# A row of exponentials times its inverse sum: the scaling of the last query tile moves from VectorE to ScalarE

## The chip, the cores and the metric

The kernel runs on one core of a Trainium2 chip. Its engines are TensorE (PE; PEld is its weight load), VectorE (DVE), ScalarE (ACT), GpSimd (POOL) and SyncE (SP), which here only issues transfers. Each works through its own queue in order and waits on semaphores for the others. The metric is the time of one execution on the device in microseconds (us).

## What is computed

Attention with rotary positions over 2 batches x 8 heads x 576 positions x 64, whose output, with the heads side by side, goes through a dense mixture of 4 experts. All in float32.

```python
scores = scale * np.matmul(q_rot, k_rot.transpose(0, 1, 3, 2))
scores = scores - np.max(scores, axis=-1, keepdims=True)
attn = np.exp(scores)
attn = attn / (np.sum(attn, axis=-1, keepdims=True) + 1e-09)
attn_out = np.matmul(attn, v)
# x: 1152 tokens x 512, p: the experts' normalised weights
for e in range(E):
    out += p[:, e:e + 1] * (np.maximum(x @ w1[e], 0.0) @ w2[e])
```

## The kernel before

Two heads are worked on together as a pair, so that each batch has four pairs. The 576 query rows of a head are 4 tiles of 128 and a rest of 64. A pair has nine units of work: units 0 to 7 are the full tiles of its two heads, and unit 8, `TAIL`, holds the 64 rest rows of both heads in one tile of 128 rows.

A unit goes through a chain. `scores` (L282, TensorE) writes a 128x576 tile to PSUM; `max` (L293, VectorE) takes the row maxima; `exp` (L301, ScalarE) writes the exponentials `e` to SBUF and adds their row sums into one column of `total`; `turn_e` and `turn_x` (L315 and L341, TensorE) transpose `e`; `high` and `low` (L332 on ScalarE, L336 on VectorE) split the transposed tile into a high and a low part, `high_x` and `low_x` (L344, L348) do so for the last 64 columns of two units; `values` (L365 to L368, TensorE) multiplies by the values; `lower` and `add` (L372 on ScalarE, L376 on VectorE) put the two halves of that product together.

Units 0 to 7 are divided by their sums only after that: `inverse` (L382, L383) turns `total` into 1/(total + 1e-9), `spread` (L392, VectorE) copies the inverses out to 512 columns, `rows` (L398, TensorE) transposes them, `divide` (L403) multiplies. Unit 8 is divided before its transposes: `scale` (L387) multiplies the SBUF tile `e` of 128x576 by the last column of `total`, one number per partition, in place. Its transposes (L315 again) wait for that; `copy_e` and `copy_x` (L351, L354) bring the result to SBUF for `tail_values` (L417).

The order of all this is written out by hand: every step has a due time in a table, `ALONE` or `BESIDE`, and one heap hands the steps to the engines' queues in order of due time. The first batch runs alone (`ALONE`); the second runs between the matmuls of the experts on the first batch's tokens (`BESIDE`; L601 to L603 with the relu L561, then L576 to L578), and the experts on the remaining tokens come last. GpSimd meanwhile rotates the queries and keys of the pairs to come and subtracts the high part of weights from the weights (L142, behind ScalarE's copy L135); towards the end it also makes sums of tokens (L644, L649) which ScalarE copies (L656). In this document "tail 1" to "tail 8" are the unit 8 of the eight pairs in order of time. Steps that belong to `TAIL` get their due times so:

```python
for key in (
    "copy_e", "copy_x", "inverse", "scale", "spread", "rows", "divide", "out_high", "out_low",
    "tail_values", "tail_high", "tail_low",
):
    at(key, getattr(self, key))
```

In `ALONE` the due times within unit 8 are exp 0.566, inverse 0.587, scale 0.712, tail_turn 1.096, spread 3.143; in `BESIDE` exp 0.181, inverse 0.243, spread 0.555, scale 0.697, tail_turn 1.093.

Of the kernel before, what the change touches and what calls it, by code (L numbers as in the profile page):

```python
# [16 lines left out]
AF = mybir.ActivationFunctionType  # L17
# [38 lines left out]
def kernel(  # L56
# [17 lines left out]
    nc = tc.nc  # L74
# [11 lines left out]
    TAIL = 2 * NR  # L86
# [58 lines left out]
    class Pair:  # L145
# [238 lines left out]

        def scale(self):
            e = self.e[TAIL]
            nc.vector.tensor_scalar_mul(e, e, self.total[:, TAIL:])  # L387

        def spread(self):
            self.rep = apool.tile([P, NR, 2, D], F32, tag="rep", name=f"rep{self.nm}")  # L390
# [727 lines left out]
```

## Time and profile before

| | |
|---|---|
| runs without a profile | 580.94, 579.58, 579.60 us; median 579.6 |
| the profiled execution | 582.67 us, of which the span of the trace is 580.9 |
| TensorE busy | 545.8 us (94%) |
| VectorE busy | 335.1 us (58%) |
| ScalarE busy | 279.1 us (48%) |
| GpSimd busy | 334.7 us (58%) |
| chain that ended last | TensorE 73%, VectorE 9%, ScalarE 8%, GpSimd 4%, transfers 3% |

The span is cut to what the engines did; 1.77 us lie around it. Busy shares are means over stages that differ: attention alone until about 107 us, attention beside experts until about 360, experts to the end. The last line follows the execution back from its last instruction, at each step to what released it.

### The profile page before, as it was taken

How to read it: one execution, taken by the hardware profiler on the slowest of the kernel's cores; microseconds unless marked ns; L12 is line 12 of the kernel's file. 1: busy time of each engine (PE TensorE's matmuls, PEld its weight loads, DVE VectorE, ACT ScalarE, POOL GpSimd, SP SyncE). 2: the span in 40 equal slices, each digit the busy share in tenths (PEclk: the TensorE clock that was granted, in tenths of full speed). 3: DMA queues.
4: the chain of work that ended last, by engine and by line, in shares of the span. 5: the costliest groups of instructions: out<-in, count | busy, mean ns of one | idle time of the engine just before them, and what ended most of it. 6: DMA issues, size and time to landing. Idle time of an engine off the chain costs nothing.

```text
span 580.9 us, 8599 instructions
## 1 busy us (share of the span) xinstructions
PE 545.8 (94%) x3229; PEld 477.9 (82%) x3229; DVE 335.1 (58%) x590; ACT 279.1 (48%) x545; POOL 334.7 (58%) x228
## 2 busy tenths in 40 slices
PE   3898888899999999999999998889999999999996
PEld 3787877788888888888888887877899899889985
DVE  5588798434362434444335445876678587777702
ACT  4688778456344554555535543443244335324400
POOL 6999992357824673478334484456663683565300
PEclk9799999999999999999999999998999999999999
DMA  5245031064125222441242124422243123223002
GB/s 149 63 120 138 3 101 60 3 184 151 66 64 157 72 74 62 113 136 49 73 136 73 45 64 140 150 54 92 74 113 106 55 77 125 73 72 109 2 0 90
DMA packets 42459, 50.67 MB, mean 87 GB/s; under 512 B 7218, under 2 KB 32050, under 8 KB 42418
## 3 DMA queue, kind: packets, MB, share of 16 engines
q1 hardware_dynamic: 41618, 49.38, 28.6%
q10 hardware_dynamic: 800, 0.75, 0.5%
q8 instruction: 25, 0.41, 0.3%
q14 instruction: 16, 0.13, 0.1%
HBM read 43.34 MB, written 2.36 MB: 79 GB/s over the span
## 4 chain that ended last, share of the span: by engine, by line
PE 73%; DVE 9%; ACT 8%; POOL 4%; DMA 3%; issue 2%; SPq 0%; ACTq 0%; POOLq 0%; DVEq 0%
PE po L816 6%; PE po L818 6%; PE po L817 6%; PE sc L282 5%; PE ph L601 4%; PE ph L603 4%; PE ph L602 4%; PE p L737 4%; PE p L738 4%; PE p L739 4%; PE po L578 4%; PE po L576 4%; PE po L577 4%; PE pp L315 4%; ACT e L301 3%
## 5 line engine op out<-in xcount | busy, mean ns | idle before, releaser
L142 POOL TENSOR_TENSOR wl<-wr,wh 128x1024 fp32r<-128x1024 f32 x64 | 155.1, 2427 | 130.6 <-ACT wh L135 125.1
L135 ACT ACTIVATE wh<-wr 128x1024 fp32r<-128x1024 f32 x64 | 67.4, 1054 | 38.8 <-PE po L578 16.6
L293 DVE TENSOR_REDUCE mx<-sc 128x1 f32<-128x576 f32 x72 | 54.2, 753 | 39.6 <-PE sc L282 39.1
L142 POOL TENSOR_TENSOR sl<-sf,sh 128x1024 fp32r<-128x1024 f32 x16 | 38.5, 2404 | 50.1 <-ACT sh L135 50.1
L816 PE MATMUL po<-wh,hH 128*128 128x512 f32 x160 | 63.0, 394 | 2.8 <-DVE hL L777 2.8
L301 ACT ACTIVATE e<-sc,mx 128x576 f32<-128x576 f32 x72 | 53.3, 741 | 24.9 <-DVE mx L293 24.4
L818 PE MATMUL po<-wh,hL 128*128 128x512 f32 x160 | 62.8, 392 | 0.0
L817 PE MATMUL po<-wl,hH 128*128 128x512 f32 x160 | 62.8, 392 | 0.0
L562 DVE SCALAR_TENSOR_TENSOR hL<-ph,hH 128x512 fp32r<-128x512 f32 x32 | 22.1, 692 | 61.0 <-ACT hH L561 61.0
L315 PE MATMUL pp<-ident,e 128*128 128x128 f32 x288 | 45.3, 281 | 7.8 <-DVE e L387 5.6
L576 PE MATMUL po<-wh,hH 128*128 128x512 f32 x128 | 52.3, 409 | 0.0
L601 PE MATMUL ph<-xH,wh 128*128 128x512 f32 x128 | 51.5, 402 | 0.0
L332 ACT ACTIVATE ptH<-pp 128x512 fp32r<-128x512 f32 x64 | 38.1, 595 | 25.3 <-PE x L365 17.2
L578 PE MATMUL po<-wh,hL 128*128 128x512 f32 x128 | 50.3, 393 | 0.0
L603 PE MATMUL ph<-xH,wl 128*128 128x512 f32 x128 | 50.2, 392 | 0.0
L577 PE MATMUL po<-wl,hH 128*128 128x512 f32 x128 | 50.0, 391 | 0.0
L602 PE MATMUL ph<-xL,wh 128*128 128x512 f32 x128 | 50.0, 391 | 0.0
L516 DVE TENSOR_TENSOR sf<-wr 128x256 f32<-128x256 f32 x32 | 39.4, 1272 | 18.3 <-DMA wr<-in_moe_w_dram 18.3
L336 DVE TENSOR_TENSOR ptL<-pp,ptH 128x512 fp32r<-128x512 f32 x64 | 43.9, 686 | 10.2 <-ACT ptH L332 9.8
L775 ACT ACTIVATE hH<-p 128x320 fp32r<-128x320 f32 x64 | 27.2, 436 | 41.0 <-DVE p L767 40.9
L135 ACT ACTIVATE sh<-sf 128x1024 fp32r<-128x1024 f32 x16 | 17.0, 1062 | 61.8 <-DVE sf L516 61.8
L315 PEld LDWEIGHTS pp<-ident,e 128*128 128x128 f32 x288 | 34.4, 143 | 14.5 <-issue 4.1
(161 smaller groups left out, 1370.9 us busy)
## 6 DMA issues: line engine op xcount, KB each, us to landing
wr<-in_moe_w_dram SPq DMA_DIRECT2D x68, 512.0 KB, 3.6
k2T<-kT SPq DMA_DIRECT2D x14, 288.0 KB, 3.9
rawv<-in_v_dram SPq DMA_DIRECT2D x8, 256.0 KB, 2.8
out_dram<-acc SPq DMA_DIRECT2D x8, 256.0 KB, 2.6
rawk<-in_k_dram SPq DMA_DIRECT2D x7, 256.0 KB, 4.2
rawq<-in_q_dram SPq DMA_DIRECT2D x7, 256.0 KB, 3.2
rawv<-in_v_dram SPq DMA_DIRECT2D x16, 32.0 KB, 2.5
tabs<-in_rope_dram ACTq DMA_DIRECT2D x1, 320.0 KB, 3.5
```

The costliest lines, as they stand in the source:

```text
L135: nc.scalar.activation(out=hi, in_=src, func=AF.Copy)
L142: eng_l.tensor_tensor(out=lo, in0=src, in1=f32(hi), op=ALU.subtract)
L315: nc.tensor.transpose(pp[:, c * P : (c + 1) * P], self.e[u][:, c * P : (c + 1) * P], ident)
L576: nc.tensor.matmul(po[t], lhsT=sH, rhs=wH, start=(f == 0), stop=False)
L577: nc.tensor.matmul(po[t], lhsT=sH, rhs=wL, start=False, stop=False)
L578: nc.tensor.matmul(po[t], lhsT=sL, rhs=wH, start=False, stop=(f == NF - 1))
L601: nc.tensor.matmul(o, lhsT=wH[:, kt], rhs=xh, start=(kt == 0), stop=False)
L602: nc.tensor.matmul(o, lhsT=wH[:, kt], rhs=xl, start=False, stop=False)
L603: nc.tensor.matmul(o, lhsT=wL[:, kt], rhs=xh, start=False, stop=(kt == KT1 - 1))
L816: nc.tensor.matmul(po[t], lhsT=sH, rhs=wH, start=(f == 0), stop=False)
L817: nc.tensor.matmul(po[t], lhsT=sH, rhs=wL, start=False, stop=False)
L818: nc.tensor.matmul(po[t], lhsT=sL, rhs=wH, start=False, stop=(f == NF - 1))
```

## The change

`scale` is issued to ScalarE as a copy with a scale per partition, in place of VectorE's multiplication. The due time stays; only the queue is another. Eight instructions change, one per pair.

```diff
         def scale(self):
             e = self.e[TAIL]
-            nc.vector.tensor_scalar_mul(e, e, self.total[:, TAIL:])
+            nc.scalar.activation(out=e, in_=e, func=AF.Copy, scale=self.total[:, TAIL:])
```

TensorE's, GpSimd's and SyncE's queues are the same instruction by instruction. On ScalarE at tail 3 (names carry the number of the pair and the unit, so `e_2_8` is the tail of pair 2; `wh` is a copy of weights):

```order
 L332 ACTIVATE ptH_2_6_1129<-pp_2_6_1124 128x4x128
 L301 ACTIVATE e_2_8_1164,total_2_843<-sc_2_8_1139,mx_2_8_1155 128x576
+L387 ACTIVATE e_2_8_1164<-e_2_8_1164,total_2_843 128x576
 L332 ACTIVATE ptH_2_6_1129<-pp_2_7_1159 128x4x128
 L135 ACTIVATE wh_0_0_1_1188<-wr_0_0_1_972 128x1024
```

The new instruction stands between the exponential of unit 8 and the high part of unit 7, with the weight copy behind that. On VectorE at tail 3:

```order
 L382 TENSOR_SCALAR total_2_843<-total_2_843 128x9
 L383 RECIPROCAL total_2_843<-total_2_843 128x9
-L387 TENSOR_SCALAR e_2_8_1164<-e_2_8_1164,total_2_843 128x576
 L293 TENSOR_REDUCE mx_3_0_1199<-sc_3_0_1172 128x1
 L336 TENSOR_TENSOR ptL_2_6_1130<-pp_2_7_1159,ptH_2_6_1129 128x4x128
```

The maxima of the next pair's first unit now follow the inverse directly. On VectorE at tail 8, in the second batch, the scaling stood behind `spread`:

```order
 L348 TENSOR_TENSOR ptX_3_6_3737<-x_112,ptX_3_6_3737 64x256
 L392 COPY rep_3_3830<-total_3_3389 128x512
-L387 TENSOR_SCALAR e_3_8_3804<-e_3_8_3804,total_3_3389 128x576
 L354 COPY at_3_8_3860<-x_112 64x128
 L376 TENSOR_TENSOR xf_3_3536<-x_112,tmp_3_3_3869 64x256
```

It no longer has `spread` in front of it; on ScalarE it stands behind L656 and ahead of `copy_e` (L351).

## Rows read from the trace of the kernel before

**Rows 1.** Stretches: length, busy us (instructions) of PE, PEld, DVE, ACT, POOL, clock, DMA.

```profile
58.00:81.00 23.00, 19.87 (x163) 17.80 (x163) 19.40 (x33) 19.21 (x46) 22.08 (x21) 1.00 0.18 44
240.00:300.00 60.00, 60.00 (x347) 51.28 (x345) 24.67 (x43) 30.05 (x56) 33.80 (x23) 1.00 0.33 98
```

**Rows 2.** Groups by line: count, busy us, mean ns, idle before and its releasers.

```profile
L387 DVE TENSOR_SCALAR e<-e,total 128x576 f32<-128x576 f32 x8 | 6.1, 766 | 0.1
...
L382 DVE TENSOR_SCALAR total<-total 128x9 f32<-128x9 f32 x8 | 7.4, 929 | 2.6 <-ACT e L301 2.5
...
L301 ACT ACTIVATE e<-sc,mx 128x576 f32<-128x576 f32 x72 | 53.3, 741 | 24.9 <-DVE mx L293 24.4
...
L406 ACT ACTIVATE xH<-xf 128x512 fp32r<-128x512 f32 x8 | 5.0, 622 | 1.1 <-DVE xf L403 1.1
```

**Rows 3.** Timeline, tail 3: start, us, engine, line, operation, [idle before <-releaser]; GpSimd, VectorE, TensorE.

```profile
77.77 2.39 POOL L142 TENSOR_TENSOR wl<-wr,wh 128x1024 fp32r<-128x1024 f32 x1
...
78.12 2.08 DVE L382 TENSOR_SCALAR total<-total 128x9 f32<-128x9 f32 x1
...
84.11 2.32 DVE L392 COPY rep<-total 128x512 f32<-128x512 f32 x1
...
87.84 0.63 PE L398 MATMUL pr<-ident,rep 128*128 128x128 f32 x4 [1.15 <-DVE ptL L336]
```

**Rows 4.** Timeline, tail 2: VectorE, ScalarE and TensorE.

```profile
56.84 1.51 DVE L387 TENSOR_SCALAR e<-e,total 128x576 f32<-128x576 f32 x1
...
59.11 0.74 ACT L301 ACTIVATE e<-sc,mx 128x576 f32<-128x576 f32 x1 [1.03 <-DVE mx L293]
...
58.40 0.66 PE L315 MATMUL pp<-ident,e 128*128 128x128 f32 x4 [0.74 <-DVE e L387]
...
61.42 0.30 PE L341 MATMUL x<-ident,e 128*64 128x128 f32 x1
```

**Rows 5.** Timeline, tail 4: VectorE and TensorE.

```profile
102.41 0.52 DVE L387 TENSOR_SCALAR e<-e,total 128x576 f32<-128x576 f32 x1
102.84 0.68 DVE L336 TENSOR_TENSOR ptL<-pp,ptH 128x512 fp32r<-128x512 f32 x1
...
104.03 0.30 PE L341 MATMUL x<-ident,e 128*64 128x128 f32 x1 [0.33 <-DVE ptX L348]
```

**Rows 6.** Timeline, tail 3 on ScalarE.

```profile
77.98 0.59 ACT L332 ACTIVATE ptH<-pp 128x512 fp32r<-128x512 f32 x1
78.46 1.07 ACT L135 ACTIVATE wh<-wr 128x1024 fp32r<-128x1024 f32 x1
...
80.28 0.38 ACT L372 ACTIVATE tmp<-x 64x256 f32<-64x256 f32 x1
81.93 0.74 ACT L301 ACTIVATE e<-sc,mx 128x576 f32<-128x576 f32 x1 [1.26 <-DVE mx L293]
```

**Rows 7.** Timeline, tail 1 on VectorE.

```profile
34.41 0.22 DVE L383 RECIPROCAL total<-total 128x9 f32<-128x9 f32 x1
...
36.01 0.68 DVE L336 TENSOR_TENSOR ptL<-pp,ptH 128x512 fp32r<-128x512 f32 x1
```

**Rows 8.** Timeline, tail 5: VectorE, ScalarE and TensorE.

```profile
170.62 0.22 DVE L383 RECIPROCAL total<-total 128x9 f32<-128x9 f32 x1
...
169.84 0.60 ACT L561 ACTIVATE hH<-ph 128x512 fp32r<-128x512 f32 x1 [0.77 <-PE ph L603]
...
172.51 0.60 PE L315 MATMUL pp<-ident,e 128*128 128x128 f32 x4
```

**Rows 9.** Timeline, tail 8: VectorE, TensorE and ScalarE.

```profile
347.01 2.00 DVE L392 COPY rep<-total 128x512 f32<-128x512 f32 x1
...
350.19 0.63 PE L315 MATMUL pp<-ident,e 128*128 128x128 f32 x4 [1.81 <-DVE e L387]
...
352.59 0.47 ACT L656 ACTIVATE t1H<-s 128x320 fp32r<-128x320 f32 x1 [0.73 <-POOL s L649]
353.72 1.06 ACT L135 ACTIVATE wh<-wr 128x1024 fp32r<-128x1024 f32 x1 [0.66 <-PE po L578]
```

## The prediction

> **What bounds the kernel now.** I began with the table of stretches, because the eight scalings do not all lie in the same kind of stage. From 240 to 300 us, where attention of the second batch runs between the matmuls of the experts, TensorE is busy for all of its 60.00 us [rows 1]: a ScalarE or VectorE instruction that comes later there costs nothing as long as TensorE's queue does not reach it. From 58 to 81 us, where attention runs alone, no engine is full: TensorE has 19.87 of 23, VectorE 19.40, ScalarE 19.21, GpSimd 22.08 [rows 1]. There the time is set by a loop of handovers (scores, maximum, exponential, transpose, high part, low part, values), and what counts is which handover ends last.
>
> Next I read the groups by line. The scaling itself, L387, takes 6.1 us in eight instructions, 766 ns each; its neighbour L382, which only adds a constant to 9 columns, takes 929 ns each [rows 2]. Nine columns can't need that. The timeline shows what it is: at tail 3 L382 starts at 78.12 and ends at 80.20, just after the GpSimd subtraction that runs from 77.77 for 2.39 us [rows 3]. So VectorE waits out a running GpSimd instruction. The scaling has the same trouble now and then: 1.51 us at tail 2 [rows 4], 0.52 at tail 4 [rows 5]. The Trainium skill (SBUF — State Buffer, section SBUF: two separate sides) says that VectorE and GpSimd hold one shared port pair as an exclusive lock for a whole instruction, and that ScalarE's ports are not part of it. By that rule the new scaling can't be held up by GpSimd, but L382 still can; the trace agrees on L382.
>
> I then went through the eight tails one by one on the timeline, asking each time what TensorE does next. I number them in order of time, 1 to 4 in the first batch (alone), 5 to 8 in the second (beside the experts).
>
> **The cost of one instruction.** The trace has no ScalarE copy of 128x576 with a scale per partition. The nearest row is the exponential over the same 576 columns, which takes one operand per partition too: 741 ns [rows 2]. From below, the plain SBUF copy of 512 columns takes 622 ns [rows 2]; from above, that of 1024 columns takes 1.07 us [rows 6]. I take 0.74, since shape and operand are those of the exponential. On ScalarE this is 8 x 0.74 = 5.9 us added, on VectorE 6.1 us removed: busy time moves, none is saved. The Trainium skill (ScalarE: Activation LUTs, section Rules for kernel authors) advises VectorE, not ScalarE, for a multiplication. Without GpSimd in the way that fits, 0.52 us being less than 0.74; by it alone the change would lose 8 x 0.22 = 1.8 us if each tail were on the path.
>
> What matters more is the order. On VectorE the scaling stood right behind the inverse, on which it depends. On ScalarE it stands right behind the last exponential, and ScalarE must now wait there, in order, until VectorE has done L382 and L383. In tails 1 to 4 the high part of unit 7 (L332), its rest (L344) and the copies behind it used to run during that wait; now they stand behind it. So each tail has a gain (the scaled tile is ready earlier if VectorE was held up in L387) and a loss (unit 7 is late).
>
> **Tail 1: 0.** The reciprocal starts at 34.41 and takes 0.22, so ScalarE can scale from about 34.68 to 35.42, and the high part, 0.59 us, follows at about 35.3 and ends at 35.9. VectorE took that part up at 36.01 [rows 7], after a maximum that does not move. So nothing is late; nothing is gained, since TensorE does not wait here.
>
> **Tail 2: -0.7.** L387 ends at 58.35 and TensorE starts the transposes of the tail at 58.40 [rows 4]. On ScalarE the scaling runs from 56.84 to 57.6: those transposes, and the scores behind them, come 0.75 earlier. The loss: on ScalarE, unit 7's high part to the copy L372 follow. At tail 3 the same sequence with a weight copy in it runs from 77.98 to 80.66, 2.68 us, of which the weight copy takes 1.07 [rows 6]; without that it is some 1.6. So ScalarE comes to the next pair's first exponential at about 59.2, where before it began at 59.11 after a wait [rows 4]: no loss worth the name. Further down TensorE's transposes at 61.42 [rows 4] wait for VectorE's copy that reads the same bank; that follows maxima that now come 0.75 earlier. I put 0.7.
>
> **Tail 3: +0.2.** Here L382 is what was long, L387 only 0.7. The inverse is done 0.25 after L382, at 80.45; ScalarE waits until then, scales until 81.2, and then has 2.68 us of work that before was done by 80.66. The next exponential starts at about 83.75 instead of 81.93 [rows 6], 1.8 late. But the path has slack: L392 starts at 84.11 and sits behind GpSimd until 86.43, and TensorE's transposes L398 come only at 87.84, after it [rows 3]. VectorE reaches L392 at about 85.1 in the new order, still inside the same GpSimd instruction, and so leaves it at the same time. I put 0.2 for what TensorE then still has to make up.
>
> **Tail 4: +0.85.** L387 took its 0.52 undisturbed, and VectorE went straight to the low part at 102.84 [rows 5], whose high part ScalarE had done in the meantime. Now: scaling 102.4 to 103.15, high part to 103.7, low part from 103.7: 0.85 later. TensorE's transposes at 104.03 [rows 5] wait for the end of this sequence, and the values and the first expert's matmuls stand behind them with no other wait. The whole amount goes through.
>
> **Tails 5 to 7: 0.** At tail 5 the inverse is done at 170.84 and TensorE comes to the tail's transposes at 172.51 without a wait [rows 8]; a scaling from 170.9 to 171.65 is in time. Behind it the next hidden layer's relu, before at 169.84 [rows 8], starts 1.7 late; what covers that is TensorE's own full queue. If that cover were gone, up to 1.7 us would be lost. At 6 and 7 the waits are shorter still, and the scaling fits in.
>
> **Tail 8: -1.0.** Here the code has L392 before L387 on VectorE. L392 starts at 347.01 and takes 2.00 us behind GpSimd; then L387; TensorE waits 1.81 us and starts at 350.19 [rows 9]. On ScalarE the scaling needs only the inverse, done long before, so TensorE goes on at about 348.2: 2.0 earlier. But this is given back in part. The weight copy on ScalarE at 353.72, which waited for TensorE and from which the next stage's weights, their load and their sums hang, stands behind L656 at 352.59, and that waited for GpSimd [rows 9]. GpSimd moves up by some 0.2 at most (no L387 in its way). So the copy gains 0.7 to 1.2, not 2.0. I take 1.0.
>
> **The sum.** 0 - 0.7 + 0.2 + 0.85 + 0 - 1.0 = -0.65 us. On the profiled execution's 582.67 that is 582.0. The runs without a profile have a median of 579.6, 3.1 lower, and spread by 1.4 among three, so I carry the difference over: 579.0. A measurement of this kernel can tell about 0.3%, 1.74 us, from no change. My forecast lies inside that.
>
> **The rivals.**
>
> *VectorE gets past GpSimd at tail 3.* If tail 2 does bring 0.7, L382 of tail 3 arrives at about 77.4, before the subtraction that starts at 77.77 [rows 3]. It then takes some 0.2 instead of 2.08, ScalarE scales early, and the next exponential comes 0.8 earlier instead of 1.8 later. L392 arrives early too and misses most of its wait: of its 2.32 us [rows 3] about 0.4 is work (an estimate from the undisturbed L387, 0.52 us for 576 columns against its 512), so 1.9 can go. I count 1.5 of that, beside the 0.7 of tail 2: -0.7 - 1.5 + 0.85 - 1.0 = -2.35, 577.2. For it: the margin is only some 0.3 us. Against: GpSimd runs through its own queue here and, with no L387 to hold it up, comes a little earlier as well, which takes that margin away again; and the runs without a profile may already have had this luck.
>
> *ScalarE's queue sets the end of each tail.* This decides if TensorE waits for the next pair's exponential rather than for the tail's transposes, and L392 finds GpSimd free, as it does at tail 4. Then the losses are 0.1 at tail 2, 1.8 at 3, 0.85 at 4, less 1.0 at tail 8: +1.75, 581.4. For it: the 1.8 us are plain in the order. Against: the long L392 at tail 3.
>
> *Everything is hidden.* Tails 4 and 8 come out equal and the others nought: 579.6. This lies in my forecast's own range, 577.9 to 580.6.
>
> **The numbers.** Forecast and the hidden case together 0.62; VectorE past GpSimd 0.24, which gives 0.25 for faster with some luck elsewhere; ScalarE's queue 0.13. The range reaches to both rivals, 577.0 to 581.3. The price of one scaling between 0.62 and 1.07 moves the four tails of the first batch by at most -0.5 to +1.3 us together, and lies inside it.
>
> **What would show it.** Right: at tail 8 no wait of TensorE for the scaled tile, its transposes about 2 us earlier, and the weight copy only about 1 earlier; at tail 4 the low part at about 103.7 counted from the same start; L382 as long as before; ScalarE waiting for L383 before L387. Wrong: if ScalarE's L387 takes over 1 us, if TensorE shows new waits for exponentials behind tails 2 and 3, or if L382 and L392 have changed places with GpSimd's instructions, in which case the chance of meeting them, and not the scaling, has set the time.

## The result, and the profile after

The changed kernel is slower: 585.82 us median (585.4 to 586.45) against 580.27 for the kernel before, a ratio of 1.0079 with a 95% interval of 1.0054 to 1.0103. Twelve more runs on another occasion gave 1.0063 (1.0040 to 1.0087). The forecast was 579.0, the range ended at 581.3. The profiled execution took 586.0 us, its span 584.2, against 582.67 and 580.9 before.

The groups by line of the changed kernel answer to [rows 2]: count, busy us, mean ns, idle before.

```profile
L387 ACT ACTIVATE e<-e,total 128x576 f32<-128x576 f32 x8 | 6.2, 777 | 8.1 <-DVE total L383 8.1
...
L382 DVE TENSOR_SCALAR total<-total 128x9 f32<-128x9 f32 x8 | 6.7, 841 | 2.6 <-ACT e L301 2.5
...
L392 DVE COPY rep<-total 128x512 f32<-128x512 f32 x8 | 8.2, 1026 | 0.1
```

The scaling takes 777 ns on ScalarE and never varies, but ScalarE stood idle for 8.1 us in front of the eight together, waiting for the inverse. L382 still takes 841 ns for its nine columns.

What went wrong is at tail 4, in the timeline of the changed kernel; it answers to [rows 5].

```profile
101.16 1.40 DVE L382 TENSOR_SCALAR total<-total 128x9 f32<-128x9 f32 x1 [0.23 <-ACT e L301]
...
102.90 0.77 ACT L387 ACTIVATE e<-e,total 128x576 f32<-128x576 f32 x1 [1.78 <-DVE total L383]
103.58 0.58 ACT L332 ACTIVATE ptH<-pp 128x512 fp32r<-128x512 f32 x1
...
104.19 0.69 DVE L336 TENSOR_TENSOR ptL<-pp,ptH 128x512 fp32r<-128x512 f32 x1 [1.39 <-ACT ptH L332]
...
103.73 0.76 PE L315 MATMUL pp<-ident,e 128*128 128x128 f32 x4 [2.14 <-ACT e L387]
105.38 0.42 PE L341 MATMUL x<-ident,e 128*64 128x128 f32 x1 [0.90 <-DVE ptX L348]
...
107.80 1.05 PE L398 MATMUL pr<-ident,rep 128*128 128x128 f32 x4
108.79 2.71 PE L417 MATMUL x<-at,rawv 128*64 128x64 f32 x20
111.42 0.50 PE L601 MATMUL ph<-xH,wh 128*128 128x512 f32 x1
```

L382 takes 1.40 us behind GpSimd (a subtraction from 100.99, for 1.54 us), the scaling runs until 103.68, and TensorE starts the tail's transposes after a wait of 2.14 us. The high part (103.58) now runs behind the scaling, the low part (104.19) behind that, and TensorE waits a second time, 0.90 us instead of 0.33. So far this is the prediction. What isn't is the length of what follows: L398 takes 1.05 us and L417 2.71, and the first expert's matmul starts at 111.42. In the kernel before, the same end of tail 4 on TensorE reads:

```profile
105.53 0.60 PE L398 MATMUL pr<-ident,rep 128*128 128x128 f32 x4
106.06 1.80 PE L417 MATMUL x<-at,rawv 128*64 128x64 f32 x20
107.79 0.50 PE L601 MATMUL ph<-xH,wh 128*128 128x512 f32 x1
```

Four transposes took 0.60 there, L417 1.80. The table of stretches (length, busy us of PE, PEld, DVE, ACT, POOL, TensorE's clock, DMA) says why; first the changed kernel, then the kernel before:

```profile
102.00:104.00 2.00, 0.27 (x2) 0.28 (x3) 0.77 (x2) 1.10 (x2) 0.53 (x1) 1.00 0.00 0
104.00:106.00 2.00, 1.10 (x6) 0.56 (x5) 1.59 (x4) 1.40 (x4) 0.00 (x0) 0.54 0.00 0
106.00:108.00 2.00, 2.00 (x10) 2.00 (x10) 0.46 (x2) 0.00 (x0) 0.00 (x0) 0.50 0.00 0
108.00:110.00 2.00, 2.00 (x15) 1.55 (x13) 1.10 (x2) 0.38 (x1) 0.00 (x0) 0.50 0.00 0
110.00:112.00 2.00, 2.00 (x15) 1.66 (x16) 0.21 (x1) 0.47 (x2) 0.00 (x0) 0.76 0.00 0
```

```profile
102.00:104.00 2.00, 0.63 (x4) 0.42 (x4) 1.90 (x6) 0.26 (x1) 0.10 (x1) 1.00 0.00 0
102.00:112.00 10.00, 8.57 (x56) 6.96 (x57) 4.57 (x12) 2.78 (x6) 1.38 (x2) 1.00 0.00 0
```

From about 104.2 to 111 us TensorE was granted 0.50, the lower of its two levels, 1.2 GHz instead of 2.4. In 102 to 104 it had been busy for 0.27 of 2 us, where the kernel before has 0.63. In the kernel before the clock stayed at 1.00 in this place.

I use one measure for this place: from the start of the accumulator read behind the tail's last exponential (L301), which is before anything the change touches, to the start of the first expert's matmul (L601).

| kernel | from | to | us | clock fell at tail 4 |
|---|---|---|---|---|
| before | 100.47 | 107.79 | 7.32 | no |
| changed | 100.93 | 111.42 | 10.49 | yes |
| changed, second profile | 101.19 | 110.78 | 9.59 | yes |
| all but tail 4 | 97.17 | 104.47 | 7.30 | no |
| tail 4 only | 99.25 | 109.74 | 10.49 | yes |
| tail 8 only | 97.58 | 104.85 | 7.27 | no |
| tails 1 to 3 only | 97.24 | 104.53 | 7.29 | no |
| before, waits filled | 95.58 | 102.88 | 7.30 | no |
| changed, waits filled | 99.92 | 108.16 | 8.24 | no |
| changed, scaling behind the high part | 97.87 | 106.45 | 8.58 | yes |
| changed, no L382 | 95.53 | 103.71 | 8.18 | yes |
| changed, no L382, waits filled | 95.55 | 102.23 | 6.68 | no |
| before, no L382 | 98.08 | 104.82 | 6.74 | no |
| changed, behind the high part, no L382 | 97.27 | 103.21 | 5.94 | no |

Five traces with VectorE's scaling at tail 4, and with L382, agree within 0.05 us. In three kernels TensorE's waits are filled with extra matmuls, which are described below.

At tail 3 of the changed kernel there is a wait that I had not seen, on ScalarE and TensorE:

```profile
81.60 0.58 ACT L236 ACTIVATE qT<-tpq 128x512 fp32r<-128x512 f32 x1
...
82.23 0.54 PE L282 MATMUL sc<-kT,qT 128*128 128x288 f32 x2 [1.28 <-ACT qT L236]
...
83.49 0.99 PE L315 MATMUL pp<-ident,e 128*128 128x128 f32 x4 [0.35 <-ACT e L301]
```

TensorE's scores for the next pair wait 1.28 us for the copy of its queries (L236), which is one of the instructions behind the scaling. After it, in this execution, the clock was down here too:

```profile
84.00:86.00 2.00, 2.00 (x11) 1.93 (x10) 2.00 (x2) 1.18 (x3) 2.00 (x1) 0.50 0.00 0
```

Tail 8, which answers to [rows 9], is as forecast:

```profile
350.19 0.77 ACT L387 ACTIVATE e<-e,total 128x576 f32<-128x576 f32 x1
...
350.40 2.00 DVE L392 COPY rep<-total 128x512 f32<-128x512 f32 x1
...
351.60 0.60 PE L315 MATMUL pp<-ident,e 128*128 128x128 f32 x4
...
354.89 0.86 POOL L649 TENSOR_TENSOR s<-s,s 128x320 f32<-128x320 f32 x1
...
355.79 0.47 ACT L656 ACTIVATE t1H<-s 128x320 fp32r<-128x320 f32 x1 [2.55 <-POOL s L649]
356.16 1.04 ACT L135 ACTIVATE wh<-wr 128x1024 fp32r<-128x1024 f32 x1
```

TensorE comes to the tail's transposes (351.60) without a wait. Counted from L398 of tail 7 (294.71 before, 298.14 after), L398 of tail 8 comes 58.59 us later instead of 60.63, 2.04 earlier, and the weight copy L135 (353.72 before, 356.16 after) 58.02 later instead of 59.01, 0.99 earlier. As forecast, it follows at once on L656, which waits for GpSimd.

In this execution that gain was lost again further on, where the clock was down from 394 to 402 us. From L398 of tail 7 to the end of the span it is 286.2 us before and 286.1 here. In the second profile of the changed kernel, with the clock down from 395 to 400 only, it is 285.1.

### The profile page after: what moved, and what is told of

It is laid out like the page before. It is cut to its first block, busy times and chain, and to the rows that moved or that the text cites. A ratio compares the mean times of both kernels' runs of the same rounds, so it can differ in the third digit from the quotient of the medians.

```text
span 584.2 us, 8600 instructions
## 1 busy us (share of the span) xinstructions
PE 552.5 (95%) x3229; PEld 483.0 (83%) x3229; DVE 333.0 (57%) x582; ACT 284.3 (49%) x553; POOL 333.5 (57%) x228
## 4 chain that ended last, share of the span: by engine, by line
PE 77%; ACT 8%; DVE 7%; POOL 5%; issue 2%; DMA 1%; ACTq 0%; POOLq 0%; DVEq 0%
PE po L816 6%; PE po L817 6%; PE po L818 6%; PE sc L282 5%; PE ph L601 5%; PE ph L603 5%; PE ph L602 5%; PE p L737 4%; PE p L738 4%; PE p L739 4%; PE po L578 4%; PE po L576 4%; PE pp L315 4%; PE po L577 4%; ACT e L301 3%; PE x L417 3%
## 5 line engine op out<-in xcount | busy, mean ns | idle before, releaser
L135 ACT ACTIVATE wh<-wr 128x1024 fp32r<-128x1024 f32 x64 | 67.4, 1053 | 36.7 <-PE po L578 16.0
L301 ACT ACTIVATE e<-sc,mx 128x576 f32<-128x576 f32 x72 | 53.3, 740 | 19.6 <-DVE mx L293 19.0
L601 PE MATMUL ph<-xH,wh 128*128 128x512 f32 x128 | 51.5, 402 | 0.0
L135 ACT ACTIVATE sh<-sf 128x1024 fp32r<-128x1024 f32 x16 | 17.0, 1061 | 62.4 <-DVE sf L516 62.4
```

The source lines that it names most:

```text
L135: nc.scalar.activation(out=hi, in_=src, func=AF.Copy)
L601: nc.tensor.matmul(o, lhsT=wH[:, kt], rhs=xh, start=(kt == 0), stop=False)
```

## The experiments

Ratios are to the kernel before, run on the same chip, with 95% intervals. Where only some tails are on ScalarE, the others are as before. Line numbers move with the edits: the scaling is also L386, L388, L390 or L392, and without the addition L382 is the reciprocal.

| kernel | ratio | interval |
|---|---|---|
| all but tail 4 | 1.0005 | 0.9979 to 1.0031 |
| tail 4 only | 1.0048 | 1.0030 to 1.0067 |
| scaling behind the high part | 0.9971 | 0.9953 to 0.9989 |
| tail 8 only | 0.9982 | 0.9965 to 0.9998 |
| changed, waits of tail 4 filled | 1.0021 | 1.0006 to 1.0036 |
| changed, no L382 | 0.9916 | 0.9900 to 0.9931 |
| before, no L382 | 0.9937 | 0.9914 to 0.9961 |
| scaling behind the high part, no L382 | 0.9904 | 0.9883 to 0.9925 |
| changed, again | 1.0063 | 1.0040 to 1.0087 |
| before, waits of tail 4 filled | 0.9999 | 0.9978 to 1.0020 |
| changed, no L382, waits filled | 0.9921 | 0.9893 to 0.9950 |
| tails 1 to 3 only | 1.0037 | 1.0018 to 1.0055 |

**Which tail.** Two kernels divide the change at tail 4.

```diff
         def scale(self):
             e = self.e[TAIL]
-            nc.vector.tensor_scalar_mul(e, e, self.total[:, TAIL:])
+            if (self.b, self.hp) != (0, NP - 1):   # the other kernel: ==
+                nc.scalar.activation(out=e, in_=e, func=AF.Copy, scale=self.total[:, TAIL:])
+            else:
+                nc.vector.tensor_scalar_mul(e, e, self.total[:, TAIL:])
```

All but tail 4:

> Scaling on ScalarE at seven tails, on VectorE at tail 4. Theory A (the loss is made at tail 4: the second wait of TensorE there, and the half clock that follows it from about 104 to 111 us in the trace of the changed kernel): without the wait and the half clock the kernel is 3 us faster than the changed one, so within 1 us of before or faster, granted clock 1.00 from 102 to 112. Theory B (the loss is ScalarE's queue at all tails, the clock a by-stander): still 3 us or more above before.

Tail 4 only:

> Scaling on ScalarE at tail 4 alone. Theory A: 3 to 5 us slower than before, with a half clock behind tail 4. Theory B: within 1 us of before.

Without tail 4 the change can't be told from no change; tail 4 alone costs 0.48%, 2.8 us, a little under the 3 to 5 that I expected. Its trace, TensorE and then the table of stretches:

```profile
102.07 0.81 PE L315 MATMUL pp<-ident,e 128*128 128x128 f32 x4 [2.14 <-ACT e L388]
103.73 0.42 PE L341 MATMUL x<-ident,e 128*64 128x128 f32 x1 [0.85 <-DVE ptX L348]
```

```profile
104.00:106.00 2.00, 2.00 (x10) 1.95 (x10) 0.62 (x3) 0.00 (x0) 0.00 (x0) 0.50 0.00 0
```

The two waits and the half clock are those of the changed kernel, and the measure is 10.49 us, the same to a hundredth. Theory A stands, as far as tail 4 goes.

**The waits or the clock.** In the changed kernel, extra matmuls of 512 columns go to TensorE's queue where it waits at tail 4; nobody reads what they write.

```diff
+        def warm(self, n, k):
+            x = banks["s"].tile([P, 2, 512], F32, f"warm{k}")
+            for i in range(n):
+                nc.tensor.matmul(x[:, i % 2, :], lhsT=identr, rhs=self.tr["k"][:, 0, 0:SM], start=True, stop=True)
...
             if u == TAIL:
+                if (self.b, self.hp) == (0, NP - 1):
+                    plan.at(t + 1.0, lambda: self.warm(8, 0))
+                    plan.at(t + 1.5, lambda: self.warm(3, 1))
                 at("tail_turn", self.turn_e, u)
```

> The changed kernel with eleven extra matmuls of 512 columns on TensorE in its two waits of tail 4 (eight before the tail's transposes, three behind them), whose results nobody reads. Theory A (the half clock behind those waits is the larger part of the loss): granted clock 1.00 from 104 to 112, the waits for the scaled tile and for the low part end when they did, and the kernel is 2 to 3 us faster than the changed one, within 2 us of before. Theory C (the waits themselves are the loss, the clock is not): as slow as the changed kernel, 4 us or more above before.

```profile
100.42 2.03 PE L384 MATMUL warm<-kT,identr 128*128 128x512 f32 x8
102.75 0.66 PE L315 MATMUL pp<-ident,e 128*128 128x128 f32 x4 [0.30 <-ACT e L392]
103.16 0.94 PE L384 MATMUL warm<-kT,identr 128*128 128x512 f32 x3
104.41 0.30 PE L341 MATMUL x<-ident,e 128*64 128x128 f32 x1 [0.30 <-DVE ptX L348]
```

```profile
102.00:112.00 10.00, 9.37 (x60) 7.08 (x60) 3.47 (x9) 4.26 (x10) 1.30 (x1) 1.00 0.00 0
```

The waits end when they did: from the exponential's end the transposes come 2.83 us later (102.75 less 99.92) where the changed kernel has 2.80. But the clock stays at 1.00, and the measure falls from 10.49 to 8.24. So of the 3.17 us that the changed kernel loses here, 0.92 are waits (8.24 less 7.32) and 2.25 the half clock; in the second profile of the changed kernel, where the clock was down for a shorter time, 1.35. Theory C falls.

The runs without a profile agree. With the waits filled the ratio is 1.0021, where the changed kernel has 1.0063 and 1.0079. The granted clock is on record as a mean for each run: over the runs it is 0.987 for tail 4 only and 0.989 for the changed kernel run again, beside 0.992 for the kernel before on the same chips, and with the waits filled it is 0.992, as before.

The Trainium skill (TensorE: Matmul & The Clock Gate, section Part 1: The HAM clock gate) ties the granted clock to how busy TensorE has been; the traces agree, since matmuls that do nothing useful held it up.

As a control, nine such matmuls (not eleven) in the kernel before:

> The kernel before with nine extra matmuls in TensorE's waits of tail 4 (eight and one). The clock did not fall there, so as a control: within 0.3% of before. If the extra matmuls themselves help or cost, it shows here.

0.9999, and the measure is 7.30: the filling by itself does nothing.

**Order or length.** The due time of the scaling in the first batch is moved, so that on ScalarE it stands behind the high part and the rest of unit 7.

```diff
-    ... inverse=0.587, scale=0.712, spread=3.143, ...
+    ... inverse=0.587, scale=1.09, spread=3.143, ...
```

> The changed kernel with the due time of the scaling in the first batch moved from 0.712 to 1.09, so that on ScalarE it stands behind the high part and the rest of unit 7 instead of ahead of them. Theory A, with ScalarE's order as the reason for the second wait: TensorE's wait for the low part of the rest (0.90 us at tail 4) goes, the clock stays at 1.00 unless the first wait alone (2.1 us) brings it down; 3 us faster than the changed kernel, or 0.9 only if the first wait is enough. Theory B with the reason in the length of the ScalarE instruction: as slow as the changed kernel.

0.9971: 0.9 to 1.1% below the changed kernel's two ratios and faster than before, though the instruction is as long and the first wait of tail 4 still 2.14 us. The second wait is gone. The clock still fell, so the measure is 8.58 and not about 7.3. So the loss of the whole change lies in the order of ScalarE's queue and not in the length of the instruction.

**Tail 8 alone**, with the condition `(self.b, self.hp) == (B - 1, NP - 1)`:

> Scaling on ScalarE at tail 8 alone. My step on tail 8 expects TensorE 2.0 us earlier at the tail's transposes and the weight copy behind it about 1.0 to 1.3 earlier, in all 1 us faster than before. The rival: the half clock near 393 us, which lasted longer in the changed kernel, comes from tail 8 being earlier, and eats the gain: 0 to 1 us slower.

0.9982, that is 1.0 us of 581.16: the forecast's step, though the interval nearly reaches 1. The rival on the half clock near 393 us is not borne out in the median, though in the first profile of the changed kernel a longer stretch there took the gain (shown above). Such a stretch lies between 384 and 402 us in all traces but one, of before too, at varying lengths.

**L382.** The sums of exponentials are at least 1, so adding 1e-9 changes no float32 among them; these kernels leave the addition out.

```diff
         def inverse(self):
-            nc.vector.tensor_scalar_add(self.total, self.total, 1e-9)
             nc.vector.reciprocal(out=self.total, in_=self.total)
```

The changed kernel without it:

> The changed kernel without L382, the addition of 1e-9 to the sums (a sum of exponentials here is at least 1, so float32 does not change by it). If what makes tail 4's wait long is L382 behind GpSimd, TensorE's first wait there falls from 2.14 to about 0.7 us, the clock stays at 1.00, and the kernel is 3 to 5 us faster than the changed one, at or below before. If the wait is made by the ScalarE instruction (0.78 us) and its place in the queue, the loss stays.

```profile
95.75 0.21 DVE L382 RECIPROCAL total<-total 128x9 f32<-128x9 f32 x1 [0.24 <-ACT e L301]
...
96.00 0.78 ACT L386 ACTIVATE e<-e,total 128x576 f32<-128x576 f32 x1 [0.28 <-DVE total L382]
...
96.83 0.66 PE L315 MATMUL pp<-ident,e 128*128 128x128 f32 x4 [0.65 <-ACT e L386]
98.49 0.30 PE L341 MATMUL x<-ident,e 128*64 128x128 f32 x1 [1.00 <-DVE ptX L348]
```

```profile
100.00:102.00 2.00, 2.00 (x13) 1.67 (x13) 0.90 (x2) 0.38 (x1) 0.00 (x0) 0.50 0.00 0
```

The reciprocal takes its 0.21 us, the first wait falls to 0.65, and the kernel is 0.84% faster than before. But the second wait, which ScalarE's order makes, is still there, and in this execution the clock fell for 3.4 us in spite of the shorter waits: my expectation that it would stay was wrong. It does not fall in every execution. Two of the five runs have a mean granted clock of 0.999 on record, which leaves about 1.2 us at the half clock in the whole of them (an estimate: 2 x 0.001 x 575 us). With five matmuls as filling:

> The changed kernel without L382 and with five extra matmuls in the waits of tail 4 (two and three). Without them its clock was at half from about 99.5 to 103.5. If extra work holds the clock up here too, 1 to 1.5 us faster than without (0.9916, so 0.989 to 0.990 of before), clock 1.00 from 98 to 104.

The clock stayed at 1.00 and the measure fell from 8.18 to 6.68, as expected, but the time is 0.9921, which the interval does not tell from 0.9916. So the 1.5 us of that one execution are not seen in the median, which fits with those two runs, in which there was no such fall to prevent.

The kernel before without L382:

> The kernel before without L382. VectorE then reaches the scaling L387 while GpSimd's instruction still runs, so by the lock the wait moves from L382 to L387 and nothing is gained: within 1 us of before. If it is the 9-column instruction alone that suffers, 1 to 3 us faster.

```profile
98.31 0.22 DVE L382 RECIPROCAL total<-total 128x9 f32<-128x9 f32 x1 [0.23 <-ACT e L301]
98.56 1.44 DVE L386 TENSOR_SCALAR e<-e,total 128x576 f32<-128x576 f32 x1
```

The wait for GpSimd moves to the scaling, as I had expected (1.44 us at tail 4, where it took 0.52), yet 0.63% are gained: I had expected nothing. Where they come from is not shown. And scaling behind the high part, without L382:

> Scaling on ScalarE behind unit 7's high part in the first batch (due time 1.09), and without L382. Should have neither of the two waits of tail 4 and no loss from ScalarE's order elsewhere: 3 us or more below before, the fastest so far. If the order does not matter any more once L382 is gone, the same as the changed kernel without L382.

```profile
98.92 0.66 PE L315 MATMUL pp<-ident,e 128*128 128x128 f32 x4 [0.99 <-ACT e L386]
```

0.9904 is the lowest ratio of all and the measure at tail 4 the shortest, 5.94 us, with one wait of 0.99 and no fall of the clock there. From the changed kernel without L382 its interval does not part it.

**The changed kernel again**, and **tails 1 to 3** (condition `self.b == 0 and self.hp < NP - 1`):

> The changed kernel once more, beside the two below. If tail 4 is nearly all of the loss (2.98 us in its trace, 2.99 in that with tail 4 alone on ScalarE, and the other seven tails 0.05%), more runs bring it down from 1.0079 towards 1.005 to 1.006. If the other tails cost something of their own, it stays at 1.008.

> Scaling on ScalarE at tails 1 to 3 alone. My steps there sum to -0.5 us. The traces of the changed kernel show a wait that I had not seen, 1.3 to 1.5 us for the copy of the next pair's queries (L236) at tail 3 and 0.6 at tail 2, but the wait for the scaled tile is shorter by as much. If these cancel: within 0.2% of before. If the queue behind the scaling costs here too: 0.2 to 0.4% slower, and the tails' sum (tail 4 +0.48%, tail 8 -0.18%) then comes to the +0.63% of the whole change.

1.0063 lies between the two cases that I had set apart, and tails 1 to 3 decide it: at 1.0037 they cost 2.1 us of their own. With tail 4 (+0.48%) and tail 8 (-0.18%) that makes +0.67%, between the two ratios of the whole change. All but tail 4 should then come to +0.19%, which its 1.0005 allows only by its interval. How tails 1 to 3 cost it is only in part shown. The trace of this kernel at tail 3:

```profile
77.91 0.66 PE L315 MATMUL pp<-ident,e 128*128 128x128 f32 x4 [0.24 <-ACT e L388]
80.08 0.53 PE L282 MATMUL sc<-kT,qT 128*128 128x288 f32 x2 [1.52 <-ACT qT L236]
```

The wait for the queries, 1.52 us here, is 1.28 to 1.52 in the five traces with L382 that have the scaling ahead of the high part at tail 3. It is in none of the four with VectorE's order there and not in the one with the scaling behind the high part, whose ratio is 0.9971. So it comes from ScalarE's order. The wait for the scaled tile is 0.24 us here; in the four traces of VectorE's order it is 0.24, 1.10, 1.59 and 1.64. So the two cancel in some executions and not in others: the trace with 0.24 (before, waits of tail 4 filled) is at the first expert's matmul at 102.88 us, this one at 104.53, and the clock was not down in either up to there. How much of the 2.1 us this makes in the median is not shown. This profiled execution is no typical one: its span is 577.8 us, its time 579.53, and the median of the runs is 583.46.

The half clock was the rival. In the first profile of the whole change the clock was down behind tail 3 (shown above), in the second behind tail 2:

```profile
62.00:64.00 2.00, 2.00 (x11) 1.93 (x10) 1.28 (x3) 0.59 (x3) 2.00 (x2) 0.50 0.00 0
```

But one profile with VectorE's order in tails 1 to 3 (tail 4 only) has such a stretch behind tail 3 as well, at 81 to 86 us, and the two kernels that share the changed order at tails 1 to 3 with VectorE at tail 4 have none, nor has the changed kernel with the waits of tail 4 filled. The clock on record for the runs speaks against it too: its mean is 0.992 with tails 1 to 3 only and in the kernel before on the same chip alike, and at the same 0.994 four runs with tails 1 to 3 took 582.92 to 583.56 us, eight of before 579.25 to 581.49. So more time at the half clock is not what makes the loss of tails 1 to 3.

## Why the prediction was wrong, point by point

**The price of one scaling**, 0.74 us, was nearly right: 0.777.

**Tail 4** is the step that failed: "0.85 later ... The whole amount goes through." The waits were nearly right, 0.92. What had no term in the sum is that TensorE, left with little to do twice in a row, would be granted half its clock for the values, the transposes and the tail's product behind them: 1.35 to 2.25 us more, shown by filling the waits. I had read the clock column of the stretches only where it stood at 1.00, though the profile of before has stretches at 0.50, from 17 to 24 and from 392 to 396 us.

**Tails 2 and 3**, -0.7 and +0.2, failed too: tails 1 to 3 measured +0.37% (0.18 to 0.55), 2.1 us, instead of -0.5 us. At tail 2 nothing came earlier: from its last exponential to that of tail 3 it is 21.5 to 22.8 us in four traces of the changed order in which the clock stayed up there, and 21.0 to 22.4 in four of VectorE's. At tail 3 I followed the exponentials, the maxima and the parts through ScalarE's queue, but not the queries' copy L236, which stands in the same queue and for which the next scores wait. The gain at the scaled tile (0.24 us of waiting, where VectorE's order has 0.24 to 1.64) goes into that wait of 1.28 to 1.52 us or is less than it. The 0.2 put for tail 3 was not worked out from a row, and no run shows it. How the 2.1 us divide stays open.

**Tails 5 to 7**, nothing: right. From the first expert's matmul (L601) to L398 of tail 5 it is 70.47 us before and 70.31 after, and from there to L398 of tail 7 116.45 and 116.41. Two slips in the working do not touch the sum: at tail 3, 81.2 and 2.68 make 83.9, not 83.75, and at tail 5 the relu would start 1.8 late, not 1.7.

**Tail 8**, -1.0 with transposes 2.0 earlier: right, 0.99 and 2.04 in the trace, 1.0 us timed alone (0.1 to 2.0, by the interval).

**The rivals.** "ScalarE's queue sets the end of each tail" had the side and the place in the order right, not the size: +1.75 us against 3.6 to 4.6, since it too knew of waits only. "VectorE gets past GpSimd at tail 3" did come about: L382 took 0.38 us at 78.50 in the changed kernel, but L392 met its 2.38 us at 83.94 all the same. In the second profile both were short (0.56 and 0.41), and its span is still 582.8 us.

**The carried difference.** One profile of before was too little to sum against. L398 of tail 3 starts at 87.84 in it, and at 82.97 to 86.66 in the three other traces that are the same program up to there. Part of that is a half clock from about 17 to 24 us, which one of these three has too, one has for half as long (18 to 22) and one has not. Another part is luck with GpSimd: L382 of tail 3 took 2.08 us and L392 2.32 in the profile that I summed against, and 0.38 to 0.97 and 0.41 to 0.80 in the other three. So what I read as the usual state of tail 3 was the exception.

## What to carry to other kernels

When an instruction moves to another engine's in-order queue, price what now stands behind its wait, all of it, and not the instruction: moved behind two others by its due time, the same instruction turned a loss of 0.6 to 0.8% into a gain of 0.3%. A wait of TensorE can have a second price, the half clock on what comes after (1.35 to 2.25 us beside 0.92 of waiting here); the clock column shows it only once it has happened, so filling the wait with unused matmuls is a way to price it. And a tiny VectorE instruction that takes 0.17 to 2.08 us is worth more attention than the large one behind it: without L382 both kernels are faster, and the change is then no loss.

## What the hardware showed that I had not expected

Whether the clock falls is not told by the length of the waits alone. With waits of 1.92 to 1.93 and 0.33 us at tail 4 it stayed up in the four traces with VectorE's order there, with L382 and no filling; with 2.13 to 2.14 and 0.85 to 1.00 it fell in three of three, with 2.14 alone it fell in the one trace, and so it did in the one with only 0.65 and 1.00. What decides it is left open. And on the same 9 columns the addition L382 takes 0.17 to 2.08 us, as GpSimd happens to run, while the reciprocal took 0.21 to 0.22 in all traces, also where no addition stood in front of it: at tail 4 of the kernel before without L382 it ran at 98.31 in the middle of a GpSimd subtraction (98.14, 1.54 us), and it was the scaling behind it that waited.
